# Decay tables from reversed reads, inputs reordered, and the last chunk routed as one group: a linear-attention and mixture-of-experts kernel on one core

## The chip, the cores and the metric

The kernel runs on one core of a Trainium2 chip. A core has five engines that run their own instruction streams and wait for each other by semaphores: TensorE (PE in the profile: matrix products and transposes, results in PSUM banks), VectorE (DVE), ScalarE (ACT), GpSimd (POOL) and SyncE (SP, which here only starts transfers). Transfers run on 16 DMA engines and are started from the queues of SyncE, ScalarE and GpSimd. The metric is the device time of one execution in microseconds (us), from the first instruction to the last.

## The reference

Two blocks follow each other. The first is a linear attention with a decaying state, for 4 batches, 8 heads, 768 tokens and 48 elements per head:

```python
state = zeros((B, H, D, D))
for t in range(S):
    kt, vt, rt = k[:, :, t], v[:, :, t], r[:, :, t]
    cur = einsum('bhd,bhe->bhde', u[None] * kt, vt)
    y[:, :, t] = einsum('bhd,bhde->bhe', rt, state + cur)
    state = w[None, :, :, None] * state + einsum('bhd,bhe->bhde', kt, vt)
```

Its output, seen as 3072 rows of 384, enters the second block: each row picks one of 4 groups by the largest of 4 logits (`x @ w_group`), then one of the 4 experts of that group (`x @ w_expert[g]`), and goes through that expert alone:

```python
h = maximum(x_rows @ w1[g, e], 0)        # 384 -> 1024
out[rows] = g_w * e_w * (h @ w2[g, e])   # 1024 -> 384; g_w, e_w: softmax weights of the choices
```

All data are 32-bit floats.

## The kernel before

The attention is worked in chunks of 128 tokens. A tile is one chunk of one batch, so there are 24 tiles: `n = 4 * chunk + batch`. The decay inside a chunk is put into two tables, `T1T` (multiplied into r, with time along the free axis) and `T2` (multiplied into k, with time along the partitions and reversed), each in three versions m = 0, 1, 2 for the position of a chunk in a span of three. Inputs come in pairs of tiles: `load_pair(g)` loads r, k and v of tiles 2g and 2g+1 into rings of four or five buffers.

The start, with cuts:

```python
load_pair(0, nc.scalar)          # r, v on SyncE's queue, k on ScalarE's
nc.scalar.dma_start(out=ub, ...) # u, spread over the partitions
load_pair(1, nc.scalar)
nc.scalar.dma_start(out=wrow, ...)
...                              # ident, flip, later made by GpSimd
nc.vector.memset(none, 0.0)
nc.scalar.copy(none[:, 0:1], ones[:, 0:1])     # ScalarE's first use
nc.vector.memset(none[:, 0:1], 0.0)
pw = bank([P, HP], "pw")
nc.tensor.transpose(pw, w2h..., ident[0:HP, 0:HP])
nc.vector.tensor_scalar(out=wc, in0=pw, ...)   # w, held within its limits
for hc in range(HP):                           # HP = 4
    nc.vector.tensor_tensor_scan(up_to[:, hc, :], wc[...], none, 1.0, OP.mult, OP.add)
nc.vector.reciprocal(by[:, 1, :], up_to[:, :, 64])
nc.vector.tensor_mul(by[:, 2, :], by[:, 1, :], up_to[:, :, P - 1])

def powers(m):       # T1T[m]: four tensor_scalar on VectorE
    for hc in range(HP):
        nc.vector.tensor_scalar(out=T1T[m][:, hc, :], in0=up_to[:, hc, :], scalar1=by[:, m, hc : hc + 1], ...)

def turned(m):       # transposed: four on TensorE, one copy on ScalarE
    ptab = bank([P, HP, P], "ptab")
    for hc in range(HP):
        nc.tensor.transpose(ptab[:, hc, :], T1T[SPAN - 1 - m][:, hc, :], ident)
    tabs[m] = pool.tile([P, HP, P], FP32, name=f"tab_{m}")
    nc.scalar.copy(tabs[m], ptab)

def flipped(m):      # time reversed: a product with a reversed identity, one copy
    ptab = bank([P, HP, P], "ptab2")
    nc.tensor.matmul(ptab..., lhsT=flip, rhs=tabs[m]..., start=True, stop=True)
    nc.scalar.copy(T2[m]..., ptab...)

powers(2); turned(0)
...                  # by[:, 0, :]
powers(0); flipped(0); powers(1); turned(1); turned(2)
```

Then the turns `s = 0 .. 28`. The engines keep the order in which the program names their instructions. Turn s works on several tiles at once; `scores(s - 1)` writes `pa` and then `am`, `values(s - 2)` writes `py` and the state `R`, `back(s - 3)` writes the rows `xt`, `rows_T(s - 4)` transposes them into `xT`, and `row_logits(s - 5)` multiplies them with the gates' weights into a bank `rb`:

```python
numbers()                                  # iotas on GpSimd
scale_k(0, nc.vector, 0, 1); scale_k(0, nc.gpsimd, 1, 2)    # kh = k * T2
for t in khs[1:] + rts[2:] + vts[2:]:      # pads of the rings
    nc.gpsimd.memset(t[:, :, :, D:DP], 0.0)
load_small()                               # five small loads on ScalarE's queue
own(0)                                     # dg = r * k * u, two multiplications on GpSimd, one buffer
for s in range(NT + LAST):                 # NT = 24, LAST = 5
    ...
    if s % 2 == 0 and s // 2 + 2 < NP: load_pair(s // 2 + 2)
    if s in (3, 5, 7, 9): zero_places(s // 2 - 1)
    run("first")
    if s < NT:
        turn(s)                            # pr, pk: transposes of r and kh; rT = pr * T1T, kT
        if s == 0: flipped(1); flipped(2)
        if s % 2 == 1 and s // 2 + 1 < NP:
            scale_k(s // 2 + 1, nc.gpsimd); own(s // 2 + 1)
    if 0 <= s - 1 < NT: own_values(s - 1)  # dv, eight on ScalarE
    run("choice")
    ...                                    # rows_T, row_logits, back, values
    if s % 2 == 0 and s // 2 < NP: own_sum(s // 2)   # du, one reduction of dg on VectorE
    if s == 2: span_decay()
    run("last")
    if 0 <= s - 1 < NT: scores(s - 1)
    if s == 0:
        for t in R: nc.gpsimd.memset(t, 0.0)
    if s == 2: late_constants()
    ...                                    # plans the parts of the routing
```

The routing of a group of tiles has five parts: `choice` (which group and expert; eight VectorE operations, one sum per tile, an exponential on ScalarE), `before` (two pairs of matmuls that count the rows ahead), `gate`, `place` (VectorE), and `rows(i)`, one scatter of 128 rows per tile into `x_sorted`, started by GpSimd. Chunks 0 to 4 are routed as groups of four tiles, the last chunk in groups of 2, 1 and 1:

```python
ROUTED = {B * c + B - 1: B for c in range(NCH - 1)}
ROUTED.update({NT - 3: 2, NT - 2: 1, NT - 1: 1})
```

Each group has its logits and small results in a bank `rb` out of two that are kept for the routing. When all rows are placed, the experts follow: `load_rows` reads an expert's rows (`xg`), `columns` transposes them (`px`, `xe`), `up` and `down` multiply (`ph`, `hT`, `po`), `rows_out` scatters to the output.

Of the kernel before, what the change touches and what calls it, by code (L numbers as in the profile page):

```python
# [15 lines left out]
P = 128  # L16
# [12 lines left out]
def kernel(  # L29
# [95 lines left out]
    def load_pair(g, k_queue=nc.sync):  # L125

        load(r, g, rts[g % RING][:, :, :, 0:D])
        load(k, g, kts[g % RING], k_queue)
        load(v, g, vts[g % (RING + 1)][:, :, :, 0:D])
# [3 lines left out]
    load_pair(0, nc.scalar)  # L133
# [5 lines left out]
    load_pair(1, nc.scalar)  # L139
    nc.scalar.dma_start(out=wrow, in_=bass.AP(tensor=w.tensor, offset=w.offset, ap=[[0, 1], [1, H * D]]))  # L140
# [8 lines left out]

    flip = cst([P, P], "flip")  # L150
    nc.gpsimd.affine_select(
        out=flip, in_=ones, compare_op=OP.is_equal, fill=0.0, base=1 - P, pattern=[[1, P]], channel_multiplier=1
    )
# [3 lines left out]
    )  # L157
    none = cst([P, P], "none")
    nc.vector.memset(none, 0.0)

    nc.scalar.copy(none[:, 0:1], ones[:, 0:1])
    nc.vector.memset(none[:, 0:1], 0.0)
# [19 lines left out]
    def powers(m):  # L182
        for hc in range(HP):
            nc.vector.tensor_scalar(
                out=T1T[m][:, hc, :], in0=up_to[:, hc, :], scalar1=by[:, m, hc : hc + 1], scalar2=None, op0=OP.mult
            )


    tabs = {}

    def turned(m):
        ptab = bank([P, HP, P], "ptab")
        for hc in range(HP):
            nc.tensor.transpose(ptab[:, hc, :], T1T[SPAN - 1 - m][:, hc, :], ident)
        tabs[m] = pool.tile([P, HP, P], FP32, name=f"tab_{m}")
        nc.scalar.copy(tabs[m], ptab)

    def flipped(m):
        ptab = bank([P, HP, P], "ptab2")
        nc.tensor.matmul(  # L200
            ptab.rearrange("p a b -> p (a b)"), lhsT=flip, rhs=tabs[m].rearrange("p a b -> p (a b)"),
            start=True, stop=True,
        )
        nc.scalar.copy(  # L204
            T2[m].rearrange("p (a e) d -> p a e d", e=2), ptab.rearrange("p a (e d) -> p a e d", e=2)[:, :, :, 0:D]
        )

    powers(2)
    turned(0)
# [3 lines left out]
    flipped(0)  # L213
    powers(1)
    turned(1)
    turned(2)

# [7 lines left out]
    def load_small():  # L225
        nc.scalar.dma_start(out=gw[:, :, 0:G], in_=moe_w_group.rearrange("(ko p) g -> p ko g", p=P))
        for g in range(G):
            nc.scalar.dma_start(
                out=gw[:, :, G + Eg * g : G + Eg * (g + 1)], in_=moe_w_expert[g].rearrange("(ko p) e -> p ko e", p=P)
            )  # L230

    iota_f = cst([P, P], "iota_f")
    tok = cst([P, NCH, B], "tok")
    region = cst([P, GE], "region")
    start0 = cst([P, GE], "start0")
    desc = cst([P, G], "desc")
    ok_i = cst([1, 1], "ok_i", I32)

    cum = cst([P, NT + 1, GE], "cum")
    nothing = cst([P, XW], "nothing")  # L240

    def numbers():
        nc.gpsimd.iota(iota_f, pattern=[[1, P]], base=0, channel_multiplier=0, allow_small_or_imprecise_dtypes=True)

        nc.gpsimd.iota(
            tok, pattern=[[P, NCH], [S, B]], base=-N, channel_multiplier=1, allow_small_or_imprecise_dtypes=True
        )

        nc.gpsimd.iota(region, pattern=[[RG, GE]], base=0, channel_multiplier=0, allow_small_or_imprecise_dtypes=True)

# [4 lines left out]
    def late_constants():  # L255
        nc.vector.tensor_scalar(out=start0, in0=region, scalar1=ident[:, 0:1], scalar2=None, op0=OP.mult)
        nc.vector.tensor_scalar(
            out=desc, in0=iota_f[:, 0:Eg], scalar1=-1.0, scalar2=float(Eg), op0=OP.mult, op1=OP.add
        )
        nc.vector.tensor_copy(cum[:, 0, :], start0)  # L260
        nc.vector.memset(nothing, 0.0)

        wlim = cst([1, H * D], "wlim")
        nc.vector.tensor_scalar(out=wlim, in0=wrow, scalar1=W_LEAST, scalar2=W_MOST, op0=OP.max, op1=OP.min)
        nc.vector.tensor_tensor(out=wlim, in0=wlim, in1=wrow, op=OP.is_equal)
        two = cst([1, 2], "two")
        nc.vector.reduce_sum(out=two[:, 0:1], in_=wlim, axis=AX)
        nc.vector.tensor_scalar(out=two[:, 1:2], in0=two[:, 0:1], scalar1=float(H * D), scalar2=None, op0=OP.is_ge)
        nc.vector.tensor_copy(ok_i, two[:, 1:2])
# [122 lines left out]

    R = ring([P, HP, P], "R", B)
# [115 lines left out]
    ROUTED = {B * c + B - 1: B for c in range(NCH - 1)}  # L509
    ROUTED.update({NT - 3: 2, NT - 2: 1, NT - 1: 1})  # L510
    GROUP = {n - i: (last, T - 1 - i) for last, T in ROUTED.items() for i in range(T) for n in (last,)}

    def row_logits(n):
        last, i = GROUP[n]
        if i == 0:
            lgs[last] = route_bank()
        logits(xTs.pop(n), lgs[last][:, NL * i : NL * (i + 1)])
# [11 lines left out]
    numbers()  # L529
    scale_k(0, nc.vector, 0, 1)  # L530
    scale_k(0, nc.gpsimd, 1, 2)
    for t in khs[1:] + rts[2:] + vts[2:]:
        nc.gpsimd.memset(t[:, :, :, D:DP], 0.0)
# [4 lines left out]
    LAST = 5  # L538
    for s in range(NT + LAST):
        if s == NT + LAST - 2:  # L540

            for t in [t for t in sorted(todo) if t > s]:
                todo[s].extend(todo.pop(t))
        pieces = todo.pop(s, [])
# [13 lines left out]
        if s < NT:  # L558
            turn(s)
            if s == 0:  # L560
                flipped(1)
                flipped(2)
            if s % 2 == 1 and s // 2 + 1 < NP:
                scale_k(s // 2 + 1, nc.gpsimd)
                own(s // 2 + 1)
        if 0 <= s - 1 < NT:
            own_values(s - 1)
        run("choice")
# [9 lines left out]
        if s % 2 == 0 and s // 2 < NP:  # L578
            own_sum(s // 2)
        if s == 2:  # L580
            span_decay()
# [3 lines left out]
        if s == 0:  # L585
            for t in R:
                nc.gpsimd.memset(t, 0.0)
        if s == 2:
            late_constants()
        if n in ROUTED:  # L590
            choice, before, gate, place, rows = routing(n)
            T = ROUTED[n]
            if n >= NT - B:
                choice()
                todo.setdefault(s + 1, []).extend(
                    [("last", part) for part in (before, gate, place)]
                    + [("last", lambda i=i, rows=rows: rows(i)) for i in range(T)]
                )
            else:
                todo.setdefault(s + 1, []).append(("choice", choice))  # L600
                todo.setdefault(s + 2, []).extend([("first", before), ("last", gate), ("last", place)])
                for i in range(T):
                    todo.setdefault(s + 3 + i, []).append(("last", lambda i=i, rows=rows: rows(i)))
    for _, part in todo.pop(NT + LAST):
        part()
    written.close()
    alive.close()
# [15 lines left out]
    nc.vector.tensor_copy(left_i, left[:, 0:1])  # L623

# [312 lines left out]
```

## Time and profile before

| what | value |
|---|---|
| time, median of 3 | 520.08 us (519.65 to 521.63) |
| span of the profiled execution | 518.1 us |
| TensorE busy | 472.7 us, 91% |
| VectorE busy | 165.1 us, 32% |
| ScalarE busy | 138.1 us, 27% |
| GpSimd busy | 124.7 us, 24% |
| mean granted TensorE clock | 0.961 |
| moved by DMA | 85.88 MB, 166 GB/s on average |

How to read the profile: it shows one execution. A row of a timeline has the start and the duration in us, the engine, the line of the program, the operation, what it writes and reads, the shapes, how many instructions are merged in it, and in brackets how long the engine was idle before it and what ended that. A row of a stretch has, for each engine, the busy time and the number of instructions, then the granted clock of TensorE, the share of the DMA engines that was busy and the GB/s moved. PEld is TensorE's loading of weights, ACTq and SPq are the queues on which transfers are started. A busy share over the whole span mixes stages with different limits, so the stages are read apart.

### The profile page before, as it was taken

The page shows a single profiled execution, that of the slowest core. Times are in us where ns is not written, and L with a number is a line of the kernel's source. Part 1 is how long each engine was busy: PE and PEld are TensorE (multiplying, and loading weights), DVE is VectorE, ACT ScalarE, POOL GpSimd, SP SyncE. Part 2 cuts the span into 40 slices and gives each one's busy share as a digit, 9 for nine tenths or more (in the row PEclk, how much of TensorE's full clock was granted, in tenths as well). Part 3 has the DMA queues.
Part 4 walks back from the last instruction along what each step waited for, and adds up shares of the span by engine and source line. Part 5 has one row for each costly group of instructions (what it writes and reads, how often), then busy time and mean ns, then how long its engine had stood idle before and what let it go on. Part 6 is the DMA issues. An engine that isn't in the chain of part 4 may idle for free. (4 is left out here: it accounts for less than half of the span.)

```text
span 518.1 us, 8753 instructions
## 1 busy us (share of the span) xinstructions
PE 472.7 (91%) x3533; PEld 454.6 (88%) x3533; DVE 165.1 (32%) x493; ACT 138.1 (27%) x400; POOL 124.7 (24%) x113
## 2 busy tenths in 40 slices
PE   1679999999999629999999999999999999999992
PEld 1568988899999518999999999999999999999992
DVE  4377577877685721011011011011011011010000
ACT  1446545555554201111111111111111111111110
POOL 1874445555543230011011011011011011011011
PEclk9889999999999657999999999999999999999997
DMA  9978989557005441564674574574574564464000
GB/s 193 221 165 206 200 194 198 142 120 279 32 34 184 152 158 42 190 244 153 191 245 156 191 246 152 191 244 150 190 246 150 190 245 151 163 225 147 1 27 26
DMA packets 110613, 85.88 MB, mean 166 GB/s; under 512 B 78475, under 2 KB 102161, under 8 KB 110566
## 3 DMA queue, kind: packets, MB, share of 16 engines
q1 hardware_dynamic: 93228, 63.71, 41.9%
q10 hardware_dynamic: 14010, 12.09, 8.8%
q0 software_dynamic: 3328, 9.47, 5.1%
q8 instruction: 29, 0.48, 0.4%
q14 instruction: 18, 0.15, 0.1%
HBM read 70.25 MB, written 15.78 MB: 166 GB/s over the span
## 5 line engine op out<-in xcount | busy, mean ns | idle before, releaser
L664 PE MATMUL ph<-xe,w 128*128 128x224 f32 x768 | 153.2, 357 | 1.1 <-DVE xe L645 1.1
L677 PE MATMUL po<-hT,w 128*128 128x224 f32 x768 | 150.7, 353 | 0.0
L664 PEld LDWEIGHTS ph<-xe,w 128*128 128x128 f32 x768 | 146.3, 193 | 1.9 <-DVE xe L645 1.4
L677 PEld LDWEIGHTS po<-hT,w 128*128 128x128 f32 x768 | 144.2, 190 | 0.0
L694 POOL DMA_INDIRECT out_dram<-yt,ids x32 | 30.6, 956 | 293.4 <-DVE yt L689 288.5
L668 ACT ACTIVATE hT<-ph 128x448 f32<-128x448 f32 x64 | 34.8, 544 | 138.3 <-PE ph L664 138.3
L689 DVE TENSOR_SCALAR yt<-pb,gates 128x384 f32<-128x384 f32 (+1 forms) x32 | 18.2, 611 | 167.0 <-PE pb L687 167.0
L680 ACT COPY yT<-po 128x224 f32<-128x224 f32 x48 | 16.6, 346 | 134.7 <-PE po L677 99.0
L416 ACT ACTIVATE dv<-vt,du 128x48 f32<-128x48 f32 x192 | 45.9, 324 | 2.2 <-DVE du L410 2.2
L645 DVE COPY xe<-px 128x448 f32<-128x448 f32 (+1 forms) x32 | 14.7, 502 | 66.5 <-PE px L642 66.5
L405 POOL TENSOR_TENSOR dg<-rt,kt 128x768 f32<-128x768 f32 x12 | 22.0, 1831 | 49.3 <-DVE du L410 49.0
L446 DVE TENSOR_TENSOR am<-pa,later 128x512 f32<-128x512 f32 x48 | 30.9, 685 | 7.0 <-PE pa L441 6.7
L441 PE MATMUL pa<-rT,kT 48*128 48x128 f32 x384 | 29.3, 288 | 2.3 <-DVE rT L429 1.5
L360 POOL DMA_INDIRECT x_sorted<-xt,place_i x24 | 23.8, 992 | 28.1 <-DVE rb L316 13.6
L463 PE MATMUL py<-am,vt 128*64 128x128 f32 x384 | 28.3, 285 | 1.8 <-DVE am L446 1.7
L441 PEld LDWEIGHTS pa<-rT,kT 48*128 48x128 f32 x384 | 24.4, 190 | 4.5 <-DVE rT L429 1.7
L463 PEld LDWEIGHTS py<-am,vt 128*64 128x64 f32 x384 | 21.9, 140 | 5.6 <-DVE am L446 2.5
L431 ACT COPY kT<-pk 128x512 f32<-128x512 f32 x24 | 14.1, 588 | 46.2 <-PE pk L427 37.6
L400 POOL TENSOR_TENSOR kh<-kt,T 128x768 f32<-128x768 f32 (+1 forms) x12 | 21.7, 1806 | 12.9 <-ACT T L204 10.9
L406 POOL TENSOR_TENSOR dg<-dg,ub 128x768 f32<-128x768 f32 x12 | 21.8, 1819 | 0.9
L457 PE MATMUL py<-rT,R 128*128 128x128 f32 x160 | 21.3, 276 | 0.4 <-DVE at L354 0.4
L389 PEld LDWEIGHTS rb<-gw,xT 128*128 128x128 f32 x144 | 19.2, 203 | 2.9 <-issue 2.9
(112 smaller groups left out, 389.2 us busy)
## 6 DMA issues: line engine op xcount, KB each, us to landing
w<-in_moe_w_dram SPq DMA_DIRECT2D x32, 1536.0 KB, 6.4
x_sorted<-nothing ACTq DMA_DIRECT2D x4, 1351.0 KB
rt<-in_r_dram SPq DMA_DIRECT2D x12, 384.0 KB, 6.4
vt<-in_v_dram SPq DMA_DIRECT2D x12, 384.0 KB, 7.7
kt<-in_k_dram SPq DMA_DIRECT2D x10, 384.0 KB, 5.7
xg<-x_sorted ACTq DMA_DIRECT2D x16, 193.0 KB, 2.6
xg<-x_sorted ACTq DMA_DIRECT2D x16, 144.8 KB, 3.4
kt<-in_k_dram ACTq DMA_DIRECT2D x2, 384.0 KB, 5.5
```

Source lines behind the costliest of these rows:

```text
L360: ins = nc.gpsimd.indirect_dma_start(out=xs_dram, out_offset=bass.IndirectOffsetOnAxis(ap=place_i[:, i : i + 1], axis=0), in_=xt[:, i, :], ...
L400: engine.tensor_mul(khs[g % (RING - 1)][:, a0:a1, :, 0:D], kts[g % RING][:, a0:a1], spread(T2[m], 1, a1 - a0))
L405: nc.gpsimd.tensor_mul(dg, rts[g % RING][:, :, :, 0:D], kts[g % RING])
L406: nc.gpsimd.tensor_mul(dg, dg, spread(ub, 1, 2))
L416: nc.scalar.mul(dv[:, h, :], vts[g % (RING + 1)][:, a, h, 0:D], dvs[g][:, a, h : h + 1])
L441: nc.tensor.matmul(pa[e][:, hc, :], lhsT=kT[rows, hc, :], rhs=rT[rows, hc, :], start=True, stop=True, skip_group_check=True,)
L446: nc.vector.tensor_mul(am[:, e], pa[e], spread(later, 1, HP))
L463: nc.tensor.matmul(py[DP * e : DP * (e + 1), hc, :], lhsT=vt[:, a, 2 * hc + e, :], rhs=am[:, e, hc, :], start=(c == 0), stop=True, skip_gr ...
L664: nc.tensor.matmul(ph[:, i, :], lhsT=w1[:, ko, P * (f + i) : P * (f + i + 1)], rhs=xe[:, ko, :], start=(ko == 0), stop=(ko == KO - 1), ski ...
L668: nc.scalar.activation(hTs[e][:, f : f + 2, :], ph, AF.Relu)
L677: nc.tensor.matmul(po, lhsT=w2[:, fo, P * d : P * (d + 1)], rhs=hT[:, fo, :], start=(fo == 0), stop=(fo == FO - 1))
L694: ins = nc.gpsimd.indirect_dma_start(out=out, out_offset=bass.IndirectOffsetOnAxis(ap=ids, axis=0), in_=yt, in_offset=None, bounds_check=N ...
```

## The change

The change has four parts.

- **Tables.** The reversal in time, which was a product with a reversed identity, is now done by reading `up_to` backwards (a step of -1) while it is multiplied. T2[m] then takes four multiplications, four transposes and one copy. Only m = 0 is made ahead of the turns; m = 1 and 2 are made at the end of turns 1 and 2. T1T is made on ScalarE.
- **Start.** `none` is no longer written by ScalarE: its first use writes a tile of its own. The first loads are named in another order on the two queues, and `wrow` is loaded later with the small loads. Constants, the pads of the rings and the zeros of R are written ahead of the first multiplications; `scale_k(1)` comes before `own(0)`, and `own_sum(0)` in turn 1.
- **Last chunk.** It is routed as one group of four, with its bank `rb` out of the six general ones; the group before it is routed one turn earlier, its four scatters in one turn.
- **End.** The comparison that decides whether rows are left over stays inside the part with a fixed order.

```diff
+    load(k, 0, kts[0], nc.scalar)
+    load(r, 0, rts[0][:, :, :, 0:D])
     nc.scalar.dma_start(out=ub..., ...)
...
-    load_pair(1, nc.scalar)
-    nc.scalar.dma_start(out=wrow, ...)
+    load(v, 0, vts[0][:, :, :, 0:D])
+    load(k, 1, kts[1], nc.scalar)
+    load(r, 1, rts[1][:, :, :, 0:D])
+    load(v, 1, vts[1][:, :, :, 0:D])
...
-    flip = cst([P, P], "flip")
...
+    # iota_f, tok, region, start0, desc, cum[:, 0], nothing: made here
+    first_use = cst([P, 1], "first_use")
+    nc.scalar.copy(first_use, ones[:, 0:1])
+    for t in khs[1:] + rts[2:] + vts[2:]:
+        nc.gpsimd.memset(t[:, :, :, D:DP], 0.0)
+    R = ring([P, HP, P], "R", B)
+    for t in R:
+        nc.gpsimd.memset(t, 0.0)
...
     def powers(m):
         for hc in range(HP):
-            nc.vector.tensor_scalar(out=T1T[m][:, hc, :], in0=up_to[:, hc, :], scalar1=by[...], ...)
+            nc.scalar.mul(T1T[m][:, hc, :], up_to[:, hc, :], by[:, m, hc : hc + 1])
+
+    def turned(m, engine_copy):
+        rev = pool.tile([P, HP, P], FP32, name=f"rev_{m}")
         ptab = bank([P, HP, P], "ptab")
         for hc in range(HP):
-            nc.tensor.transpose(ptab[:, hc, :], T1T[SPAN - 1 - m][:, hc, :], ident)
-    ...
-    def flipped(m):
-    ...
+            src = up_to[:, hc, :]
+            back = bass.AP(tensor=src.tensor, offset=src.offset + P - 1, ap=[list(src.ap[0]), [-1, P]])
+            nc.vector.tensor_scalar(out=rev[:, hc, :], in0=back, scalar1=by[:, SPAN - 1 - m, hc : hc + 1], ...)
+            nc.tensor.transpose(ptab[:, hc, :], rev[:, hc, :], ident)
+        engine_copy(T2[m]..., ptab...)
-    powers(2)
-    turned(0)
+    turned(0, nc.vector.tensor_copy)
...
     powers(0)
-    flipped(0)
-    powers(1)
-    turned(1)
-    turned(2)
...
-    ROUTED = {B * c + B - 1: B for c in range(NCH - 1)}
-    ROUTED.update({NT - 3: 2, NT - 2: 1, NT - 1: 1})
+    ROUTED = {B * c + B - 1: B for c in range(NCH)}
...
-            lgs[last] = route_bank()
+            lgs[last] = route_bank() if last < NT - 1 else bank([P, 512], "rb")
...
     scale_k(0, nc.gpsimd, 1, 2)
+    scale_k(1, nc.gpsimd)
     load_small()                 # now with wrow
     own(0)
...
+    def todo_for(n, s):
+        choice, before, gate, place, rows = routing(n)
+        lag = 1 if n < NT - B - 1 else 0
+        todo.setdefault(s + lag, []).append(("choice", choice))
+        todo.setdefault(s + lag + 1, []).extend([("first", before), ("last", gate), ("last", place)])
+        for i in range(B):
+            at = s + 3 + i if lag else s + 1
+            todo.setdefault(at, []).append(("last", lambda i=i: rows(i)))
...
+        for n in range(NT):
+            if s == max(n + 1, 2):
+                own_values(n)
...
-        if s % 2 == 0 and s // 2 < NP:
+        if s % 2 == 0 and 0 < s // 2 < NP:
             own_sum(s // 2)
-        if s == 2:
-            span_decay()
+        if n in ROUTED:
+            todo_for(n, s)
+            if n == NT - B - 1:
+                run("choice")
         run("last")
         if 0 <= s - 1 < NT:
             scores(s - 1)
-        if s == 0:
-            for t in R:
-                nc.gpsimd.memset(t, 0.0)
-        if s == 2:
-            late_constants()
...
+        if s == 1:
+            own_sum(0)
+        if s in (1, 2):
+            turned(s, nc.scalar.copy)
+            powers(s)
+        if s == 3:
+            span_decay()
+        if s == 6:
+            check_decay()
+    todo[NT + LAST - 1][-1][1]()
+    for _, part in todo[NT + LAST]:
         part()
-    written.close()
-    alive.close()
...                               # the comparison for rows left over
+    written.close()
+    alive.close()
```

## The prediction

> **What bounds the kernel now.** I read the slices of the page first, then the stretches between 0, 44, 172, 195 and 518 us, then the timeline of the two stretches in which TensorE is not full.
>
> ```profile
> PE   1679999999999629999999999999999999999992
> ...
> PEclk9889999999999657999999999999999999999997
> ```
>
> Each digit is 13 us. TensorE is full from the fourth slice to the thirteenth and again from the sixteenth on.
>
> ```profile
> 0.00:44.00 44.00, 26.00 (x233) 20.74 (x234) 24.27 (x66) 16.43 (x49) 22.77 (x31) 0.92 0.98 192
> 44.00:172.00 128.00, 124.76 (x1546) 115.57 (x1544) 90.53 (x231) 68.97 (x232) 63.54 (x42) 1.00 0.61 156
> 172.00:195.00 23.00, 8.36 (x35) 7.18 (x35) 11.86 (x77) 1.30 (x7) 7.81 (x8) 0.53 0.49 166
> 195.00:518.00 323.00, 313.57 (x1722) 311.07 (x1722) 38.43 (x122) 51.45 (x112) 30.61 (x32) 0.98 0.49 166
> ```
>
> First busy column: TensorE. The attention turns (44 to 172) and the experts (195 on) have it 97% busy and the change hardly touches them. It is idle for 18 us of the head and 14.6 us of the seam between attention and experts. These 33 us are all that the change can draw on. The head, by its timeline:
>
> ```profile
> 3.22 3.09 ACTq L140 DMA_DIRECT2D wrow<-in_w_dram  x1
> ...
> 6.34 1.28 ACT L161 ACT_TABLE_LOAD   x1 [6.34 <-issue]
> 7.63 0.19 ACT L161 COPY none<-ones 128x1 f32<-128x1 f32 x1
> 7.87 0.16 DVE L171 TENSOR_SCALAR wc<-pw 128x4 f32<-128x4 f32 x1 [5.17 <-issue]
> ...
> 11.37 0.59 ACT L196 COPY tab<-ptab 128x512 f32<-128x512 f32 x1 [3.55 <-PE ptab L194]
> ...
> 14.19 0.48 ACT L204 COPY T<-ptab 128x384 f32<-128x384 f32 x1 [2.23 <-PE ptab L200]
> ...
> 23.37 1.82 POOL L400 TENSOR_TENSOR kh<-kt,T 128x768 f32<-128x768 f32 x1
> ...
> 25.25 1.12 PE L427 MATMUL pk<-ident,kh 128*128 128x128 f32 x4 [3.91 <-POOL kh L400]
> ```
>
> ScalarE issues wrow for 3.09 us, then loads its table, then writes one column of none; VectorE has to clear that column again before wc, though pw was done at 5.11. The first table T2 is ready only at 14.67. Later the second pair's scaled k waits on GpSimd behind own(0) and the state memsets.
>
> ```profile
> 31.00 1.82 POOL L405 TENSOR_TENSOR dg<-rt,kt 128x768 f32<-128x768 f32 x1 [0.35 <-DVE w_span L252]
> 31.03 1.82 DVE L253 TENSOR_TENSOR w_span<-w_span,up_to 128x4 f32<-128x4 f32 x1
> ```
>
> A VectorE operation on four elements takes 1.82 us, to the very end of a GpSimd multiplication. The seam:
>
> ```profile
> 181.49 0.17 DVE L313 TENSOR_REDUCE mx<-rb 128x5 f32<-128x20 f32 x1
> ...
> 185.85 0.16 DVE L356 CAST place_i<-rb 128x1 uint32<-128x1 f32 x1
> 186.79 0.97 POOL L360 DMA_INDIRECT x_sorted<-xt,place_i  x1 [0.54 <-issue]
> 189.81 5.10 ACTq L633 DMA_DIRECT2D xg<-x_sorted  x8
> ```
>
> The last tile's choice starts at 181.49 because three groups of the last chunk follow each other on VectorE and take turns at two route banks; the experts' rows are read 2.05 us after the last scatter ends (187.76).
>
> [...] The trace agrees (1.82 us above; the 16-element tensor_scalar of start0 took 0.66 us, to a GpSimd end). [...] The trace shows 0.50 from 24 to 30 us and from 174 to about 200; at the very start the record reads 1.00 although the first two flip matmuls took 2.05 us and four later ones 1.88. [...] The first three slices move 193, 221 and 165 GB/s here.
>
> **The change part by part.** *Input order*: taken queue by queue it is the same order (w, r0, v0, r1, v1 on SyncE; k0, u, k1 on ScalarE); only wrow goes later. So 0 us by itself, but ScalarE is free at about 3.2 and its table load ends near 4.7.
>
> *First table.* VectorE no longer waits for ScalarE: wc at 5.25 instead of 7.87 gives 2.6 us. The constants now made ahead of it (start0 0.2, desc 0.15, cum 0.17, nothing 0.38) fit before 5.25. From wc to the factors 1.98 us as now, so 7.23; four reversed multiplications 0.9 (T1T x4 now 0.88), 8.1; last transpose 0.6, 8.7; copy on VectorE 0.55 (my choice, like the 0.55 of xt), 9.3. Tab copy 0.59 and flip 2.05 are gone. T2[0] at 9.3 instead of 14.67: **5.4 us earlier**.
>
> *First turns.* powers(0) now on ScalarE: dv with 48 elements costs 1.91/8 = 0.24 each; copies of 512 and 384 elements (0.59, 0.47) give 0.94 ns per element, so 0.31 each for 128, 1.3 us, done at 11.0. Then six small DMA issues instead of five (0.40 + 2.12 now, so 3.0) stand ahead of kT(0): 14.1 to 14.7. scores(0) follows at 14.7 instead of 19.59: 4.9 us earlier. GpSimd has done the pads and R memsets (1.8 + 1.9) in idle time, scales pair 1 first, and ends own(0) at about 16.4 instead of 21.55.
>
> *Given back.* The tables for m = 1, 2 now sit in turns 1 and 2, in one chain: am(0) to 17.2, du(0) 0.95 to 18.2, four reversed reads 0.9, transposes 0.6, and only then turn(2). Their VectorE operations run beside own(1), own(2), whose single dg buffer starts them the moment du is read. At best the four take 0.9 us; if GpSimd gets the port between any two of them, up to 2 x 1.83 = 3.7 us more each time (two multiplications, then GpSimd itself must wait). And TensorE idles about 2.5 us there, so part of turn(2) and values(0) is at half clock. Step by step: turn(2) 1.3, values(0) 1.7, scores(1) 1.2, am(1) 1.3, reversed reads and transposes 1.5, turn(3) 1.3, back 0.6, values(1) 1.7, scores(2) 1.2 (14 us with hand-overs of 2), then 4.1 to scores(3). From 19.5, where the first transposes end, that makes 35.4 without the hand-overs and 37.4 with them, against 42.61 now: 5.2 to 7.2 us, middle 6.2. Half clock and port waits of 0 to 5 us come off; I take 1.2, nearer to none because four independent operations in a row should mostly keep the port. **Head: 5.0 us.** After scores(3) both kernels are TensorE bound at the same step. The late constants (about 2.9 us of VectorE at 34 to 37) only explain part of the 42.61; I don't count them again.
>
> *Seam.* the choice for tiles 16 to 19 moves one turn ahead, beside values(22) and scores(23): am(23) 0.4 later, the two "before" matmuls 0.7 in TensorE's stream, but yT(23) no longer waits for the exponential (170.39 to 170.05), pb(23) 170.9, xt 172.1, px 172.7, rb(23) ends 174.1 warm or 174.9 cold. One pass for four tiles, from the pass at 166.90: choice 2.92, exponential 0.35, gate 1.06, place 0.65, so 4.95 in all: 179.1 to 179.9. From place to scatter 0.77 (now 186.01 to 186.79). Four scatters at 1.285 apart and 0.97 for the last: end at 184.7 to 185.5 instead of 187.76. **Seam: 2.6 us.** The three short passes it replaces cost more VectorE time, but what counts is that the four scatters, formerly nearly done when the last place came, now all follow it: 3.9 us given back.
>
> Sum: 5.0 + 2.6 = 7.6, from 520.1 to **512.5 us**.
>
> **Rivals.** (a) *The port becomes the bound of turns 1 and 2*: reversed reads alternate with GpSimd's multiplications, TensorE goes cold, the head gives 1 us, the whole 516.5. For: w_span; against: there the second operation depended on the first, here four independent ones stand in a row. (b) *All warm and no lock* [...]: head 9, whole 508.5. For: the late constants are off turn 2; against: a clock of 0.50 at 24 to 30 now. (c) *Transfers*: an earlier start meets the same 200 GB/s, and the zero fills (1.35 MB each) come sooner, so later turns would wait for r, k, v. For: SyncE's issues take 4 to 8 us at 45 to 73; against: no TensorE wait on a DMA from 44 to 172, and from 30 to 32 us no DMA runs at all, so there is some room. It would leave about 517. (d) *Seam unchanged*, as scatters in a row after the last place eat the pass saved: 515.
>
> **Range and chances.** Head 1 to 9, seam 1.5 to 3.5, and 1 us either way for the clock's phase at the first expert: 508 to 517. Over 2% faster means under 509.7: 0.2. Same 0.78, slower 0.02.
>
> **What would show it.** T2[0] written at 9 to 9.5; the first pa at 14 to 15.5; the rev rows of turns 1 and 2 either at 0.2 each or at up to 2 us each (rival a); pa of turn 4 at 36 to 40; no tab, no flip; one mx of 128x80 near 174.5 less the head's gain; four scatters 1.28 apart as the last before xg. Wrong if TensorE waits on DMA between 40 and 80 us, or if kT(0) comes much later than 14.7 because the small DMAs' issues are slow.

## The result and the profile after

| | before | changed |
|---|---|---|
| time, median | 520.24 us (519.65 to 521.63) | 528.67 us (525.94 to 529.38) |
| ratio to before, 95% interval | | 1.0148, 1.0106 to 1.0191 |
| span of the profiled execution | 518.1 us | 527.6 us |
| scores of turn 0 begin | 19.59 us | 21.02 us |
| scores of turn 3 | 42.61 us | 49.23 us |
| scores of turn 23, the last | 164.51 us | 176.25 us |
| first transpose of the experts' rows | 192.44 us | 201.82 us |

The kernel became slower, by 1.5%. The starts of the scores, read from TensorE's timeline, say where. For turn 3, the last turn and the experts' first transpose, in the kernel before:

```profile
42.61 1.16 PE L441 MATMUL pa<-rT,kT 48*128 48x128 f32 x16
164.51 1.16 PE L441 MATMUL pa<-rT,kT 48*128 48x128 f32 x16
192.44 1.59 PE L642 MATMUL px<-ident,xg 128*128 128x128 f32 x6 [7.99 <-DMA xg<-x_sorted]
```

and in the changed one:

```profile
49.23 1.16 PE L430 MATMUL pa<-rT,kT 48*128 48x128 f32 x16
176.25 1.16 PE L430 MATMUL pa<-rT,kT 48*128 48x128 f32 x16
201.82 1.51 PE L627 MATMUL px<-ident,xg 128*128 128x128 f32 x6 [12.57 <-DMA xg<-x_sorted]
```

So 1.4 us are lost by turn 0, 6.6 by turn 3, 11.7 by the last turn, and of these 2.4 come back in the seam. From the first expert on both traces take 325.7 to 325.8 us.

The slices of the page after, TensorE's busy tenths and its granted clock:

```profile
PE   1459989999999916999999999999999999999992
...
PEclk9988979999999955999999999999999999999997
```

The second and third slices have fallen (4 and 5 after 6 and 7), and in the sixth (66 to 79 us), full before, there is now a dent in the busy time (8) and in the clock (7). The stretches, cut at 44 us as in the prediction and then where the seam now lies:

```profile
0.00:44.00 44.00, 19.02 (x137) 15.98 (x139) 25.81 (x48) 13.91 (x45) 20.72 (x29) 0.92 1.14 154
44.00:182.00 138.00, 133.48 (x1635) 123.80 (x1631) 100.05 (x254) 72.54 (x245) 64.35 (x42) 0.98 0.68 153
182.00:204.50 22.50, 6.13 (x36) 4.88 (x35) 6.69 (x37) 1.35 (x6) 8.81 (x9) 0.60 0.61 196
```

TensorE works 19.0 us of the first 44, not 26.0. The last two columns of the first row are the surprise: the DMA engines are busier (1.14 after 0.98; the share adds up the times of all packets, so it can pass 1) and move less (154 GB/s after 192). The head's timeline after:

```profile
3.65 3.63 DVE L173 TENSOR_SCALAR start<-region,ident 128x16 f32<-128x16 f32 x1 [1.09 <-POOL region L172]
...
5.29 1.96 POOL L189 MEMSET R<- 128x512 f32 x4
...
7.94 0.10 DVE L198 TENSOR_SCALAR wc<-pw 128x4 f32<-128x4 f32 x1
...
11.40 0.56 DVE L224 COPY T<-ptab 128x384 f32<-128x384 f32 x1 [0.62 <-PE ptab L223]
...
14.06 6.27 ACTq L244 DMA_DIRECT2D gw<-in_moe_w_expert_dram  x4
...
20.38 1.07 ACT L420 COPY kT<-pk 128x512 f32<-128x512 f32 x2 [6.01 <-DMA gw<-in_moe_w_expert_dram]
21.02 1.14 PEld L430 LDWEIGHTS pa<-rT,kT 48*128 48x128 f32 x10 [5.02 <-ACT kT L420]
```

Two waits that the prediction didn't have. The operation start0, on 16 elements, stands from 3.65 to 7.28, to the end of GpSimd's eleven memsets (3.56 to 7.25), so wc comes at 7.94, no earlier than before. And ScalarE spends 6.27 us on issuing four small loads, with kT(0) behind them. Turn 1, the reversed products:

```profile
25.19 3.99 DVE L220 TENSOR_SCALAR rev<-up_to,by 128x128 f32<-128x128 f32 x4
25.35 1.81 POOL L394 TENSOR_TENSOR dg<-rt,kt 128x768 f32<-128x768 f32 x1 [6.50 <-DVE du L399]
...
27.24 1.87 POOL L395 TENSOR_TENSOR dg<-dg,ub 128x768 f32<-128x768 f32 x1
```

Four products that took 0.87 us ahead of the turns (9.90) last until GpSimd has ended both of its multiplications (29.11); in turn 2 they take 2.87 us (36.67 to 39.54; GpSimd's end at 39.26). This is what the prediction and the expectations call the port: VectorE operations that go on to the end of a GpSimd one. The traces show the times, not what in the chip makes them so. Turn 6, where the change has put the decay check (clip wrow and compare):

```profile
64.47 1.82 POOL L395 TENSOR_TENSOR dg<-dg,ub 128x768 f32<-128x768 f32 x1
64.63 2.06 DVE L256 TENSOR_TENSOR wlim<-wlim,wrow 1x384 f32<-1x384 f32 x1
...
67.55 0.67 DVE L418 TENSOR_TENSOR rT<-pr,T1T 128x512 f32<-128x512 f32 x1
68.27 1.62 PE L430 MATMUL pa<-rT,kT 48*128 48x128 f32 x16 [1.68 <-DVE rT L418]
```

and the stretch that follows, TensorE's clock in the third column from the right:

```profile
72.00:76.00 4.00, 4.00 (x22) 3.77 (x20) 0.56 (x1) 2.49 (x10) 0.00 (x0) 0.50 1.36 190
```

The check's second operation holds VectorE to the end of a GpSimd multiplication (66.29) and a little longer; rT(7) comes late, TensorE idles 1.68 us, and from 72 to 76 us its clock is halved (0.50). The two steps of the scores around it take 7.62 and 9.82 us, in the kernel before 5.87 and 6.45: 5.1 us. The seam:

```profile
185.59 0.24 DVE L304 TENSOR_REDUCE mx<-rb 128x20 f32<-128x80 f32 x1 [2.11 <-PE rb L380]
...
187.56 0.98 POOL L351 DMA_INDIRECT x_sorted<-xt,place_i  x1 [0.30 <-issue]
...
191.60 0.16 DVE L347 CAST place_i<-rb 128x4 uint32<-128x4 f32 x1 [1.30 <-DMA x_sorted<-xt,place_i]
...
196.38 0.98 POOL L351 DMA_INDIRECT x_sorted<-xt,place_i  x1 [0.30 <-issue]
...
199.17 5.04 ACTq L618 DMA_DIRECT2D xg<-x_sorted  x8
```

One choice, one place, four scatters, as designed. But the new place_i must wait 1.30 us for the scatter that started at 187.56, the last one of chunk 3, which the order of turns had put behind the four of chunk 4.

### The profile page after: what moved, and what is told of

It reads as the page before. It is cut to its first block, busy times and chain, and to the rows that moved or that the text cites. A ratio compares the mean times of both kernels' runs of the same rounds, so it can differ in the third digit from the quotient of the medians.

```text
span 527.6 us, 8687 instructions
## 1 busy us (share of the span) xinstructions
PE 472.4 (90%) x3519; PEld 455.9 (86%) x3519; DVE 170.8 (32%) x459; ACT 139.3 (26%) x404; POOL 124.4 (24%) x112
## 5 line engine op out<-in xcount | busy, mean ns | idle before, releaser
L630 DVE COPY xe<-px 128x448 f32<-128x448 f32 (+1 forms) x32 | 14.7, 502 | 67.3 <-PE px L627 67.3
L627 PE MATMUL px<-ident,xg 128*128 128x128 f32 x96 | 12.8, 269 | 12.6 <-DMA xg<-x_sorted 12.6
L627 PEld LDWEIGHTS px<-ident,xg 128*128 128x128 f32 x96 | 11.1, 146 | 13.6 <-issue 12.7
```

Source lines behind the costliest of these rows:

```text
L627: nc.tensor.transpose(px[:, i, P * j : P * j + n], xg[0:n, j, P * ko : P * (ko + 1)], ident[0:n, 0:n])
```

## The experiments

The theory formed from these lines: four separate waits, each put in by one part of the change (constants, small loads, reversed products, decay check), and beside them slower transfers, for which no line gave a reason. The rival: the transfers are the cause, and the four waits would only be traded for waits on r, k and v. Each result is given as median of the kernel, median of the kernel before on the same chip beside it, and ratio with its 95% interval.

### Both kernels once more

Nothing edited.

> The kernel before, unchanged, for a second profile. If the slower transfers of the changed kernel's head come from the change, this one shows 200 to 240 GB/s from 8 to 24 us, as its first profile; if the rate differs by run or chip, it shows 150 to 190 as the changed kernel and its variants do. The time is that of the kernel before, ratio 1.00.

521.33 against 520.66 us, 1.0009 (0.9993 to 1.0024). Between 8 and 24 us it moves 209 to 230 GB/s.

> The changed kernel, unchanged, beside the others of this set: ratio 1.015 to the kernel before, and the rates of its head 150 to 190 GB/s from 8 to 24 us if they come from the change.

530.51 against 520.66 us, 1.0181 (1.0145 to 1.0216), and 153 to 188 GB/s again: the lower rate belongs to the change. So single edits of the changed kernel are to be held against 1.015 to 1.018.

### The decay check, to the end

```diff
-        if s == 6:
-            check_decay()
...
     for _, part in todo[NT + LAST]:
         part()
+    check_decay()
```

> The changed kernel with its six VectorE operations of check_decay moved from turn 6 to after the last routing; nothing else. Theory A ([...] TensorE idles 1.7 us for rT and then runs turn 7 at half clock): the step from scores(5) to scores(6) falls from 7.6 to about 5.9 us and the next from 9.8 to about 6.5, so the time is about 5 us below the changed kernel's 528.7, near 523.6. Rival B (late inputs hold turns 6 and 7 up, the check only happens to stand there): no more than 1 us.

525.63 against 522.56 us, 1.0040 (1.0019 to 1.0060). The two steps are back at 5.87 and 6.44 us, and the clock stays at 1.00 from 62 to 78 us. A one-row comparison in the wrong turn cost about 1.1 to 1.4%.

### The small loads, one turn later

```diff
-    load_small()
     own(0)
...
         if s == 1:
+            load_small()
             own_sum(0)
```

> The changed kernel with the six small loads on ScalarE's queue moved from ahead of own(0) to the end of turn 1. Theory A (their issue keeps ScalarE for 7 us [...], so kT(0) is late by about 5 us and with it the first scores): kT(0) starts near 15 instead of 20.4, scores(0) at 15 to 16 instead of 21.0, and the time falls by 3 to 5 us, to 524 to 526. Rival B (the head is held by the rates of the transfers or by own(0) on GpSimd, which ends at 18.9): scores(0) comes earlier but scores(2), now at 44.35, by less than 2 us.

523.85 against 522.56 us, 1.0028 (1.0007 to 1.0048). kT(0) is written at 14.73, not 20.38, and the scores of turn 0 begin at 16.33. What is left of the delay is the late wc (with both gone, in e7_all below, they begin at 13.46).

### The constants, one turn later

```diff
-    (start0, desc, cum[:, 0], nothing: ahead of wc)
...
+        if s == 0:
+            (start0, desc, cum[:, 0], nothing)
```

> The changed kernel with start0, desc, the first column of cum and nothing written at the end of turn 0 instead of ahead of wc; nothing else. wc then starts at about 4.9 to 5.3 instead of 7.94, and T2[0] is written near 9. Theory A (the small loads' issue holds kT(0) whatever comes before it[...]): kT(0) starts at 19 to 21 as now, time within 1 us. Rival B (the issue takes its 6.3 us from wherever it starts): kT(0) at about 17.5, time 2 to 3 us lower.

528.20 against 522.02 us, 1.0101 (1.0029 to 1.0173). wc comes at 4.91 and the first table is copied at 8.55 to 9.11, as predicted. But the small loads then take 7.31 us to issue (11.61 on), kT(0) is written at 18.97, and most of the gain is gone. Of two waits in a row, taking away the first alone shows little.

### The reversed products of turns 1 and 2 on ScalarE

```diff
+            if m == 0:
                 nc.vector.tensor_scalar(out=rev[:, hc, :], in0=back, scalar1=by[...], ...)
+            else:
+                nc.scalar.mul(rev[:, hc, :], back, by[...])
```

> The changed kernel with the reversed multiplications of m = 1 and 2 on ScalarE instead of VectorE; the place in the order is the same. Theory A [...]: about 1.3 us for four on ScalarE, scores(2) 3 to 4 us earlier, the time 3 to 4 us lower, near 525. Rival B (it is their place in the chain, not the port): the four take as long as the engine before them lets them, scores(2) moves by under 1.5 us.

522.46 against 522.56 us, 0.9981 (0.9955 to 1.0007), the largest effect of one edit and well above what was expected. ScalarE makes the four of turn 1 in 1.28 us; the scores of turn 3 begin at 42.01, not 49.23.

```profile
22.41 1.28 ACT L225 ACTIVATE rev<-up_to,by 128x128 f32<-128x128 f32 x4
...
26.43 1.82 POOL L397 TENSOR_TENSOR dg<-rt,kt 128x768 f32<-128x768 f32 x1 [7.57 <-DVE du L402]
```

GpSimd's multiplications are only half of it. GpSimd is idle while these four run, and they end 5.5 us earlier than in the changed kernel (23.69 after 29.18): 2.7 us because they are shorter, 2.8 because ScalarE starts them before VectorE would have come to them. So the second explanation, their place in the order, has its share. In turn 2 they do run beside a GpSimd multiplication (31.58 and 31.87) and take 1.28 us again.

### The last scatter of chunk 3, one turn earlier

```diff
-            at = s + 3 + i if lag else s + 1
+            at = s + 3 + min(i, 1 if n == NT - 2 * B - 1 else i) if lag else s + 1
```

> The changed kernel with the last scatter of chunk 3 named one turn earlier, so that GpSimd starts it before the four of chunk 4 instead of after them; nothing else. Theory A (the last chunk's places are written into the buffer that this scatter reads, and wait 1.3 us for it): the conversion to place_i follows its sum at once and the experts begin 1.3 us earlier. Rival B (the scatters of chunk 4 hold it anyway, or GpSimd is busy until then): within 0.3 us.

527.46 against 520.66 us, 1.0125 (1.0095 to 1.0155). place_i no longer waits; from the last scores to the experts' first transpose 24.5 us pass, after 25.6 in the changed kernel and 27.9 in the one before.

### The kernel before with the new routing alone

Only ROUTED, todo_for, the bank and the end from the change; head, tables and loads as before.

> The kernel before with only the routing part of the change: last chunk as one group of four with its bank among the six, the group before it one turn earlier, its four scatters in one turn. The head is that of the kernel before. From the traces the seam gains 2.4 us (experts begin 25.6 us after the last pa in the changed kernel, 27.9 in the one before), so 518.2 against 520.6, ratio 0.995. Rival: the gain belongs to the other phase of the changed kernel and is gone, ratio 1.000.

519.20 against 522.02 us, 0.9954 (0.9928 to 0.9980). The same stretch takes 25.3 us: the seam's 2.6 us stand. This kernel's transfers are slow too (137 to 175 GB/s between 8 and 24 us), though its head and its loads are those of the kernel before. So neither the order of loads nor the reversed reads slow them. What it shares with the changed kernel is that tiles have gone or shrunk, and the rings of r, k and v lie elsewhere.

### Where the rings lie

r and v arrive in pieces of 192 bytes (48 numbers of a head) at steps of 256 (DP = 64), so all pieces of a kernel begin at the same distance from a multiple of 256. Four kernels move the rings by a tile that nobody uses or by a wider one:

```diff
# e5_pad, 32 bytes          -first_use = cst([P, 1], "first_use")  +first_use = cst([P, 16], "first_use")
# e8_addr, 2656 bytes       +cst([P, 664], "shift")
# e10_a64, 64 bytes         +cst([P, 16], "shift")
# e11_b64, 64, in before    +cst([P, 16], "shift")
```

> The changed kernel with first_use 16 columns wide instead of one, so that the rings of r, k and v stand at 32 bytes past a multiple of 64, as in the kernel before, instead of on a multiple. It looks for the cause of the slower transfers of the head (163 GB/s from 10 to 14 us at a DMA share of 1.48, against 237 at 1.17 before). Theory A (the places of the rings set the rate): 220 to 240 GB/s from 10 to 20 us, small loads issued in about 3 us, time 2 to 5 us lower. Rival B (the rate differs from run to run or by other causes): time within 1 us of the changed kernel's and the rate low, or high in other runs of this set too.

> The changed kernel with an unused tile of 2656 bytes per partition ahead of the rings, so that the rings of r, k and v stand at exactly the addresses they have in the kernel before; nothing else. Theory A (the places of the rings make the transfers of the head slow): 210 to 240 GB/s from 8 to 24 us as before, the small loads issued in 2 to 3 us, time 525 or less. Rival B (what the engines do at that time, or which transfers stand beside each other, makes them slow): 150 to 190 GB/s and a time within 1 us of the changed kernel's.

> The changed kernel with 64 more bytes ahead of the rings of r, k and v, so that every 192-byte piece of r and v begins 0 bytes after a multiple of 256 instead of 192, and none crosses a multiple of 256. Theory 'pieces that cross a multiple of 256 bytes are slower to write': the transfers move 205 to 235 GB/s between 8 and 24 us (the changed kernel 153 to 188), scores of turns 0 and 2 begin at 17.6 and 40.8 us (21 to 22 and 44 to 45), the experts' first transpose at about 198.5, the time is about 523 (against 528 to 530 for the changed kernel). Rival 'the area of the memory, some kilobytes further on, makes the difference, not the last 256 bytes': 150 to 190 GB/s, 22 and 45 us, 528 to 530 as without it. Rival 'it differs from one execution to the next': either, without order.

> The kernel before with 64 more bytes ahead of the rings: pieces of r and v begin 96 bytes after a multiple of 256 instead of 32, and every one crosses a multiple of 256. Theory of the crossings: the rate between 8 and 24 us falls from 208 to 239 GB/s to 140 to 180; scores of turn 0 begin at 20 to 21 us; the time is 0 to 3 us above the kernel before, because the kernel before waits little for transfers in these turns. Rivals: 208 to 240 GB/s as before, time unchanged.

| kernel | a piece begins at (mod 256) | crosses a multiple of 256 | GB/s in the four stretches of 4 us from 8 to 24 | ratio (interval) |
|---|---|---|---|---|
| before | 32 | no | 217, 239, 208, 221 | 1 |
| changed | 192 | yes | 175, 159, 154, 161 | 1.0148 |
| e5_pad | 224 | yes | 175, 157, 149, 155 | 1.0132 (1.0071 to 1.0192) |
| b_tail | 160 | yes | 175, 157, 164, 137 | 0.9954 |
| e8_addr | 32 | no | 232, 217, 192, 208 | 1.0026 (1.0000 to 1.0051) |
| e10_a64 | 0 | no | 231, 218, 199, 214 | 1.0028 (1.0010 to 1.0046) |
| e11_b64 | 96 | yes | 172, 156, 162, 138 | 1.0013 (0.9995 to 1.0031) |

The places are the addresses, in bytes of a partition, at which the compiled programs put the rings. e5_pad rested on a first guess, a step of 64 bytes: by that measure its pieces stood as in the kernel before, and neither rate nor time improved. Sixty-four bytes turn the rate on in one kernel and off in the other. The stretches, the changed kernel first, DMA share and GB/s at the end of the row:

```profile
12.00:16.00 4.00, 2.64 (x14) 2.42 (x12) 2.60 (x5) 1.28 (x4) 3.96 (x3) 1.00 1.47 159
16.00:20.00 4.00, 0.40 (x2) 0.00 (x0) 0.27 (x1) 0.00 (x0) 2.77 (x2) 1.00 1.50 154
```

The changed kernel with 64 bytes more:

```profile
12.00:16.00 4.00, 2.64 (x14) 2.42 (x12) 2.60 (x5) 1.28 (x4) 3.95 (x3) 1.00 1.14 218
16.00:20.00 4.00, 2.48 (x18) 1.79 (x17) 0.51 (x2) 1.07 (x2) 2.81 (x2) 1.00 1.23 199
```

The kernel before with 64 bytes more:

```profile
12.00:16.00 4.00, 3.29 (x9) 2.18 (x10) 1.90 (x8) 1.40 (x3) 0.64 (x1) 1.00 1.31 156
16.00:20.00 4.00, 4.00 (x19) 2.99 (x18) 0.69 (x1) 1.57 (x4) 4.00 (x9) 1.00 1.46 162
```

Busier engines that move less: more time per piece. The traces hold a record of every piece. Put in the order of SyncE's queue, from its second load up to 24 us, a piece of r or v takes 15 to 18 ns in the mean of a load in e8_addr, e10_a64 and the kernel before, and 24 to 30 ns in the other four. But crossing alone is not slow. k's pieces lie end to end, without gaps; two or three of every four cross a multiple of 256 in every kernel, and in those first three they take 15 to 16 ns, too (among the slow pieces of the others, 19 to 25 from the second load of k on). And r's first load takes 15.5 to 19.6 ns per piece in the four kernels where it crosses, 16.4 to 17.5 in the three where it does not. What has to come together with a crossing is open; below, rings are called aligned where pieces of r and v begin at 0 or 32.

By the distance from a multiple of 256 the rate does not fall step by step: the kernels of the table know two levels, 192 to 239 GB/s at 0 and 32, and 137 to 175 at 96, 160, 192 and 224 (over all runs the levels touch: in single stretches 186 with aligned rings, 193 without). What in a transfer takes the longer time, no trace shows.

Why it costs time shows in e10_a64 at the small loads:

```profile
14.09 2.89 ACTq L245 DMA_DIRECT2D gw<-in_moe_w_expert_dram  x4
17.02 1.07 ACT L421 COPY kT<-pk 128x512 f32<-128x512 f32 x2 [2.64 <-DMA gw<-in_moe_w_expert_dram]
```

The same four issues take 2.89 us where they took 6.27 (and 7.44 in c_after): ScalarE gets away sooner. Scores of turn 0 begin at 17.66. The low rate alone doesn't make the issues slow: in e11_b64 they begin 2.9 us later than in the changed kernel and take 2.26 us. With aligned rings no run shows more than 2.9, with the others 2.3 to 7.6. What the queue had still to do at each time isn't shown. In the kernel before the same loss of rate (e11_b64) costs nothing that the interval could show, though in the trace the scores of turn 3 begin at 45.9 after 43.3 in c_before.

### The edits together

Five edits at once: constants, small loads, ScalarE's reversed products, decay check, scatter.

> The changed kernel with five edits together: check_decay after the last routing, the small loads at the end of turn 1, start0, desc, cum and nothing at the end of turn 0 instead of ahead of wc, the reversed multiplications of m = 1 and 2 on ScalarE, chunk 3's last scatter one turn earlier. If the costs are the ones named and lie one behind the other: 528.7 less 5.0 (check), 6.4 (small loads), 7.8 (reversed reads; measured singly 4.7, 6.4, 7.8, here with some overlap), 2.0 (constants) and 1.3 (scatter), that is 508 to 512, ratio 0.975 to 0.985. If they hide each other or the transfers hold the head: 515 to 519.

514.09 against 520.66 us, 0.9872 (0.9850 to 0.9894). Now faster than before, but the small loads, at the end of turn 1, hold ScalarE from 13.58 to 21.67, and so the first reversed products, which begin at 21.72.

The same, with the small loads at the end of turn 2 and the constants in turn 4:

> As the version with five edits, but the small loads at the end of turn 2 instead of turn 1, nothing written right after the first table, and start0, desc and the column of cum in turn 4 ahead of own_sum. In the five-edit version ScalarE stood 7.6 us at those loads before the reversed reads of m = 1 (21.7). Theory A (that is what holds turns 2 and 3): those reads start near 17.5, scores(3) at about 36.5 instead of 40.4, time near 510.5. Rival B (own(0) and own(1) on GpSimd and the transfers hold them): scores(3) not before 39, time 513 to 514.

515.95 against 522.02 us, 0.9880 (0.9820 to 0.9941), above both expectations. The wait moved: they are issued from 24.60 to 32.65, and the next kT (35.20) waits 8.96 us. Putting the issue later didn't help here.

Both with the 64 bytes:

> The five edits together (constants and small loads later, two of four reversed products on ScalarE, decay check at the end, last scatter of chunk 3 one turn earlier), and the 64 bytes. Theory of the crossings: rate 200 to 240 GB/s between 8 and 24 us, the small loads' issue (13.6 to 21.7 us) shrinks by 2 to 3 us, scores of turns 1 and 2 begin 2 to 4 us earlier than 27.5 and 35.6; time 508 to 512. Rivals: 148 to 193 GB/s, 514 as without the bytes.

509.88 against 521.41 us, 0.9785 (0.9755 to 0.9815), with all products of m = 1 and 2 on ScalarE, as in e7_all.

> The same, but with the small loads at the end of turn 2 and the constants in turn 4, and the 64 bytes. Theory of the crossings: rate 200 to 240 GB/s between 8 and 24 us; scores of turns 2 and 3, which waited for the late small loads (29.3 and 41.9 us), begin 2 to 4 us earlier; time 510 to 514. Rivals: 157 to 188 GB/s, 516 as without the bytes.

507.22 against 521.41 us, 0.9745 (0.9713 to 0.9777): the fastest version, with all parts of the change in it. The small loads take 3.3 us to issue (24.83 to 28.09), the scores of turns 0 to 3 begin at 13.47, 20.50, 28.50 and 33.70. So the first theory stands for the four waits, and the rival is right in part: the 64 bytes alone are worth 1.2 to 1.5% in the changed kernel, as much as one of the waits, and until the transfers were mended, a part of what was gained at one wait was lost again at the small loads (e3_const, e7_all, e9_later).

### Do the losses add?

The 64 bytes and the decay check at the end, nothing else:

> The changed kernel with the 64 bytes and with the decay check at the end, nothing else. Theory that these two losses add: steps from turn 5 to 7 of 5.9 and 6.4 us instead of 7.6 and 9.8, so the experts' first transpose at about 192.8 (with the 64 bytes alone 197.9) and the time about 518, that is 0.5% below the kernel before. Rival 'with the transfers mended, the check falls beside other work': 520.5 or more, and no more than 2.5 us below the kernel with the 64 bytes alone.

521.06 against 520.91 us, 1.0011 (0.9991 to 1.0032). The trace follows the first theory (steps of 5.87 and 6.44 us, experts' first transpose at 193.15), the time the rival: only 2 us below e10_a64 by the medians, 1 us by the ratios. The executions of both kernels spread over 5 to 6 us (521.2 to 526.1 and 519.5 to 525.5), and the one whose trace was taken for e10_a64 was among its longest, so its 197.87 is probably too late for a typical one. All nine traces with the check in turn 6 show a stretch of half clock after it (one product py<-rT,R takes 1.91 or 1.92 us there, not 1.06), and none of the seven in which it stands at the end (1.06 to 1.16 between 60 and 80 us). Why the time still gains so little stays open. With these two losses gone the changed kernel equals the one before; the rest of the head still eats the seam's gain.

The fastest version with the four reversed products back on VectorE:

> The quickest kernel so far (507.2 us) with all four reversed products of turns 1 and 2 on VectorE again, as in the change. Theory that they take turns with GpSimd's products at the port: the four take 2.8 to 4 us in each of the turns, scores of turn 2 begin 3 to 6 us later than 28.5, and the time is 511 to 514. Rival 'without the small loads and the late constants around them they fit into idle time': 507 to 508.5, scores of turn 2 at 28.5 to 29.5.

515.93 against 520.91 us, 0.9892 (0.9867 to 0.9916): 1.5% or some 7.7 us more than with ScalarE by the ratios. The scores of turn 2 begin at 36.29, not 28.50. Turn 1 in this kernel:

```profile
15.26 1.29 DVE L431 TENSOR_TENSOR am<-pa,later 128x512 f32<-128x512 f32 x2 [1.84 <-PE pa L426]
16.47 0.94 DVE L395 TENSOR_REDUCE du<-dg 128x16 f32<-128x768 f32 x1
17.33 3.99 DVE L215 TENSOR_SCALAR rev<-up_to,by 128x128 f32<-128x128 f32 x4
17.49 1.81 POOL L390 TENSOR_TENSOR dg<-rt,kt 128x768 f32<-128x768 f32 x1 [1.46 <-DVE du L395]
```

and in the fastest version:

```profile
14.06 1.28 ACT L220 ACTIVATE rev<-up_to,by 128x128 f32<-128x128 f32 x4
14.21 1.81 POOL L394 TENSOR_TENSOR dg<-dg,ub 128x768 f32<-128x768 f32 x1
```

The products end at 21.32 instead of 15.34. Of these 6.0 us 2.7 are the products' own length (3.99 after 1.28): on VectorE they last to the end of GpSimd's second multiplication (21.24), on ScalarE they run beside one (14.21 to 16.02) and take 1.28 us, as long as in turn 1 of e4_rev, where GpSimd is idle. The other 3.3 are the later start, because on VectorE they stand behind am(0), which waits for the scores, and du(0). And du is also what lets GpSimd start the next multiplication: in all eleven traces with the products of turn 1 on VectorE they meet it and take 4.0 us.

## Why the prediction was wrong

It said 512.5 us and the kernel took 528.7. By its steps:

- **"The constants now made ahead of it (start0 0.2, ...) fit before 5.25": failed.** start0 took 3.63 us, and wc came at 7.94. The prediction had noted that this very operation lasted to a GpSimd end in the kernel before (0.66 us) and GpSimd's pads and zeros of R "in idle time", and did not put the two side by side. With the constants elsewhere wc came at 4.80 to 4.97 and T2[0] at 9.1, and the step's own working (9.3) holds.
- **"Six small DMA issues ... so 3.0": failed as a size.** They took 7.2 us (13.10 to 20.33), and kT(0) came at 20.4 instead of 14.1 to 14.7. With aligned rings the six took 3.9 (13.11 to 16.98 in e10_a64) and 3.3 in e13_later64: nearer to the estimate, so most of the miss goes with the slower transfers. Its closing remark, that slow issues would make it wrong, named the place.
- **"Four independent operations in a row should mostly keep the port": failed.** Rival (a) is what happened, 3.99 and 2.87 us. Its size, "the whole 516.5", is nearly that of e15_rev0 (515.9), where of the four waits only this one is left; the fastest version (507.2), without it, answers to rival (b), 508.5.
- **"Input order: 0 us by itself": the rate was taken as given.** No run tests the order alone, but b_tail shows that the slow transfers don't come from it. Tiles taken out of the program moved the rings by 2656 bytes, and the transfers lost a quarter of their rate. Rival (c) had transfers as waits for r, k and v between 40 and 80 us; they came instead as longer issues on ScalarE, at 14.
- **The decay check: left out.** The prediction counted late constants as gone from turn 2 and did not follow where their other half went. In turn 6 it met GpSimd's multiplication (2.06 us for one operation) and then half clock (0.50 from 72 to 76 us), about 5 us in the traces and 1.1 to 1.4% by e1_check.
- **Seam, 2.6 us: right.** 2.4 in the changed kernel, 2.6 in b_tail; choice to the end of place took 6.2 us with the wait of 1.30 in it, so about 4.9 without (predicted 4.95). The wait for chunk 3's last scatter was missed; without it the seam gains 3.4.

The head's single effects overlap: the ratios of e1, e2, e3, e4 and e10 each save 0.5 to 2%, from the mean of the two ratios of the changed kernel (1.0165) 6.5% in sum, but e13_later64, with the scatter too, saves 4.2%, probably because small loads and slow transfers are in part the same wait, and the constants' gain is lost in it. The range failed because its width came from the clock and from VectorE's waits on GpSimd alone; every step's start was taken from the step before, without going through each engine's queue for what else now stood in it.

## What to carry to other kernels

Moving an operation in an engine's order moves the wait with it: for each one moved, list what stands behind it in its own queue and, for VectorE and GpSimd, what the other does in those microseconds (here VectorE's operations went on to GpSimd's end and took 3.63, 3.99 and 2.06 us). When tiles are added or removed, look where the others have moved to: where pieces of 192 bytes with gaps between them crossed multiples of 256, the head of this kernel lost a quarter of its rate (154 to 175 GB/s after 208 to 239), and 64 bytes of padding brought it back (199 to 231). Where several waits stand in a row, single edits mislead; try them together.

## What was not expected of the hardware

- The place of the destination within 256 bytes set the rate: pieces of 192 bytes at steps of 256 at 0 or 32 past a multiple of 256 moved at 192 to 239 GB/s, at 96, 160, 192 and 224 at 137 to 175 with busier engines (8 to 24 us of the kernels in the table). Pieces of k, which lie end to end, took 15 to 16 ns in the faster kernels, as long as those of r and v, though two or three of four cross.
- The time that ScalarE needed to issue four small loads went from 2.1 us (before) over 2.9 (e10_a64) to 7.4 (c_after); what else sets it besides the rate is open.
- A VectorE operation on 16 elements, which takes 0.42 us in e12_all64, took 3.63 us while eleven GpSimd memsets followed each other (3.56 to 7.25); it did not end between two of them. Between the two GpSimd multiplications of turn 1 an operation did: the third of the four products ran there, from 27.16 to 27.44.
- An idle time of TensorE of 1.68 us in otherwise full work was followed by half clock (0.50) from 72 to 76 us; in e1_check, without it, the clock read 1.00 from 62 to 78.
